# Maxima stored as eight rows, spread by a matmul for the second batch, and a new opening order, in an attention and feed-forward kernel

## The chip, the cores and the metric

The kernel runs on one core of a Trainium2 chip. The metric is the time of one execution on the device in microseconds (us); three executions of the kernel before were timed, and one more was profiled.

## What is computed

Eight batches of eight heads, 576 tokens, head size 64, go through an attention over 32 "memories" per head, and the result goes through a feed-forward network whose two weight matrices arrive as 64-bit floats.

```python
a = exp(phi - max(phi, axis=2)); a = a / sum(a, axis=2)      # phi: 8 x 8 x 576 x 32, over the tokens
k_m, v_m = a^T k, a^T v                                        # 32 memories per head
attn = softmax(q k_m^T / 8)                                    # over the 32 memories
x = (attn v_m), heads side by side: 4608 x 512
h = x @ w_in                                                   # 512 x 2048
out = (h * clip(h + 3, 0, 6) / 6) @ w_out                      # 2048 x 512
```

## The kernel before

**The tiling.** The product of a batch's `v_m` with `w_in` is formed once for each batch (`fold`, four chunks of 512 columns), so that the first large matmul multiplies softmax probabilities with it. The work after that is cut into slots, one for each batch and each 128 of the 2048 columns. A slot has the words `g` (12 matmuls into the tile `ph`, L427), `u` (ACT: relu of h + 3, L437), `m` (DVE: clip and product, L443), `h` and `l` (split of the result into a high and a low part, ACT L456 and DVE L461) and `a` (12 matmuls into the tile `acc`, L481). Slots 0 to 7 are "plain" halves with 4 records for `g` and 4 for `a`. From slot 8 on there are 12, so slot 20 begins with the 177th record of L427 (32 + 12 x 12 + 1), and slot 40, the first that the steady table lays out, with the 369th (slots 36 to 39 have no `g`).

**The order.** Nothing is scheduled by the machine. The string `BEGIN` lists words one after another for slots 0 to 39 of the first two batches; `play` calls the function of each word, and each call appends its instructions to the queue of its engine. Every engine works its own queue strictly in that order. From slot 40 on the table `STEADY` gives the same pattern for each batch. All loads and stores are issued on SP's queue; there too a transfer that must wait holds up all that follow it.

**The attention words** that matter here, with batch and half behind them: `pt`, `pn` load the two layouts of phi (the tiles `ptile` and `pnat`), `kv` a piece of keys and values, `q` the queries. `mx` takes the maxima over the tokens on DVE (L220). Batch 0 spreads them to all partitions on chip: `md` makes two diagonal matrices on DVE (L236), `me` multiplies them by ones on PE (L240). Batches 1 to 7 go through DRAM: `mo` stores the 128 x 2 maxima (L225), `sp` loads them into every partition (L230) and must wait until `mo` has landed. `xa` adds the negated maxima to `pnat` (DVE, L245), `xe` is the exponential (ACT, L249), `kvm` the memories (PE, L257), `nr`, `nk`, `tp`, `tk` normalise and turn them, `sc` the scores (PE, L295), `ct`, `cm`, `cs`, `ex`, `ds`, `dr`, `dm`, `bt` the softmax (`cs` subtracts the maximum, L325; `dm` multiplies by the inverse sum, L337; both on DVE for the first half of batch 0, else on POOL), `bh` and `bl` split the probabilities (`bl`: L350, DVE or POOL as for `cs`). `fo` is the fold (PE, L362), `vc`, `vh`, `vl` copy and split it.

**The weight words.** Weights come as raw 64-bit words (`raw` for a 512 KB piece of `w_in`, `raw2` for a 1 MB unit of `w_out`) and are turned into 32-bit floats by `ab` (ACT, L132), `ro` (ACT, L136), `cl` (DVE, clamp, L140), `sh` (DVE, shift, L143), `si` (DVE, sign, L148) and a final add, which is `tg` on POOL or `to` on DVE (both L158). `sx` and `sy` split a unit of `w_out` into a high part (ACT, L165) and a low part (POOL, L169). `wk` keeps a finished chunk of `w_in` in DRAM. The pieces of `w_in` for chunks 1 to 3 and the pieces of keys and values share one ring of five buffers. `warm` is a matmul that does no work.

Of the kernel before, what the change touches and what calls it, by code (L numbers as in the profile page):

```python
# [729 lines left out]
```

## Time and profile before

| what | us |
|---|---|
| three timed executions, median (lowest to highest) | 755.34 (751.94 to 755.71) |
| the profiled execution, its own time | 754.04 |
| its span, first to last instruction | 752.2 |
| PE busy in it | 718.6 |
| DVE busy | 390.7 |
| ACT busy | 325.8 |
| POOL busy | 113.1 |

PE is busy for 96% of the span, but that share is an average. From some 140 us on it is at work without a gap; before that it waits. Rows of a timeline give the start, the length and the engine of an instruction, and in brackets how long its engine had been idle and what ended that.

### The profile page before, as it was taken

The page shows a single profiled execution, that of the slowest core. Times are in us where ns is not written, and L with a number is a line of the kernel's source. Part 1 is how long each engine was busy: PE and PEld are TensorE (multiplying, and loading weights), DVE is VectorE, ACT ScalarE, POOL GpSimd, SP SyncE. Part 2 cuts the span into 40 slices and gives each one's busy share as a digit, 9 for nine tenths or more (in the row PEclk, how much of TensorE's full clock was granted, in tenths as well). Part 3 has the DMA queues.
Part 4 walks back from the last instruction along what each step waited for, and adds up shares of the span by engine and source line. Part 5 has one row for each costly group of instructions (what it writes and reads, how often), then busy time and mean ns, then how long its engine had stood idle before and what let it go on. Part 6 is the DMA issues. An engine that isn't in the chain of part 4 may idle for free.

```text
span 752.2 us, 11547 instructions
## 1 busy us (share of the span) xinstructions
PE 718.6 (96%) x4754; PEld 565.6 (75%) x4758; DVE 390.7 (52%) x576; ACT 325.8 (43%) x625; POOL 113.1 (15%) x74
## 2 busy tenths in 40 slices
PE   7886958999999999999999999999999999999997
PEld 3334637778887878787887878787887878888885
DVE  3897878675635355345543354444543455343332
ACT  2565646555433344443443434343433434343331
POOL 1352633133200021002200021002200022000000
PEclk9998998999999999999999999999999999999999
DMA  9948873549523080816263080816264211130002
GB/s 322 408 49 317 244 226 135 202 140 229 190 83 126 15 332 3 154 58 247 86 69 143 16 320 13 144 69 218 117 49 161 72 57 57 57 112 1 1 1 70
DMA packets 26453, 99.85 MB, mean 133 GB/s; under 512 B 4513, under 2 KB 5409, under 8 KB 21793
## 3 DMA queue, kind: packets, MB, share of 16 engines
q1 hardware_dynamic: 26400, 99.12, 42.8%
q8 instruction: 37, 0.61, 0.3%
q14 instruction: 16, 0.12, 0.1%
HBM read 83.38 MB, written 15.74 MB: 132 GB/s over the span
## 4 chain that ended last, share of the span: by engine, by line
PE 84%; DMA 8%; DVE 5%; issue 1%; ACT 1%; SPq 0%; DVEq 0%; ACTq 0%
PE acc L481 51%; PE ph L427 26%; DMA raw<-in_w 5%; PE pv L362 4%; PE pk L257 2%; DVE tmp L148 2%; DMA pnat<-in_pn 1%; PE psc L295 1%; DMA qh<-in_qt 1%; DVE tmp L140 1%; DVE tmp L143 1%; DVE both L382 0%; DVE gf L443 0%; ACT tmp L132 0%; DVE glo L461 0%
## 5 line engine op out<-in xcount | busy, mean ns | idle before, releaser
L481 PE MATMUL acc<-w,ghi 128*128 128x512 f32 x1120 | 295.2, 401 | 0.0
L481 PEld LDWEIGHTS acc<-w,ghi 128*128 128x128 f32 x1120 | 205.1, 189 | 68.4 <-ACT gf L437 15.1
L427 PE MATMUL ph<-phi,both 128*128 128x256 f32 x992 | 177.1, 300 | 17.5 <-DVE gf L443 11.7
L443 DVE SCALAR_TENSOR_TENSOR gf<-gf,ph 128x576 f32<-128x576 f32 x124 | 93.4, 753 | 191.4 <-ACT gf L437 191.4
L437 ACT ACTIVATE gf<-ph,three 128x576 f32<-128x576 f32 (+2 forms) x132 | 95.8, 726 | 216.6 <-PE ph L427 213.6
L427 PEld LDWEIGHTS ph<-phi,both 128*128 128x128 f32 x992 | 151.5, 190 | 34.2 <-DVE gf L443 14.1
L481 PE MATMUL acc<-w,glo 128*128 128x512 f32 x560 | 158.1, 395 | 0.0
L481 PEld LDWEIGHTS acc<-w,glo 128*128 128x128 f32 x560 | 105.7, 189 | 25.0
L461 DVE TENSOR_TENSOR glo<-gf,ghi 128x512 fp32r<-128x512 f32 x124 | 88.3, 712 | 44.9 <-ACT ghi L456 41.4
L427 PE MATMUL ph<-plo,both 128*128 128x256 f32 x496 | 107.8, 299 | 0.0
L456 ACT CAST ghi<-gf 128x512 fp32r<-128x512 f32 x124 | 76.4, 616 | 13.6 <-PE acc L481 6.7
L427 PEld LDWEIGHTS ph<-plo,both 128*128 128x128 f32 x496 | 81.0, 192 | 0.0
L382 DVE TENSOR_TENSOR both<-pv,both 128x512 fp32r<-128x512 f32 x62 | 42.5, 689 | 48.6 <-ACT both L373 48.6
L325 POOL TENSOR_TENSOR st<-st,mx 128x640 f32<-128x640 f32 (+1 forms) x15 | 21.8, 1457 | 300.1 <-DVE mx L321 293.3
L447 ACT COPY rest<-gf 128x64 f32<-128x64 f32 x124 | 30.2, 245 | 84.1 <-DVE gf L443 84.1
L373 ACT CAST both<-pv 128x512 fp32r<-128x512 f32 x62 | 35.9, 584 | 25.3 <-DVE both L382 17.4
L362 PE MATMUL pv<-w,kvT 64*32 64x512 f32 (+1 forms) x528 | 36.9, 588 | 1.5 <-DVE w L158 1.3
L350 POOL TENSOR_TENSOR plo<-pT,phi 128x640 fp32r<-128x640 f32 (+1 forms) x15 | 22.2, 1478 | 63.3 <-ACT phi L345 63.3
L337 POOL TENSOR_TENSOR st<-st,sm 128x640 f32<-128x640 f32 (+1 forms) x15 | 19.0, 1267 | 63.8 <-DVE sm L333 61.9
L148 DVE SCALAR_TENSOR_TENSOR tmp<-raw,tmp 128x512 uint32<-128x512 uint32 (+1 forms) x24 | 26.4, 1130 | 0.3
L132 ACT ACTIVATE tmp<-raw 128x512 f32<-128x512 f32 (+1 forms) x24 | 19.1, 832 | 15.4 <-DMA raw<-in_w 12.3
L257 PE MATMUL pk<-kvt,pnat 128*32 128x129 f32 (+1 forms) x640 | 21.5, 276 | 2.4 <-ACT pnat L249 1.7
(64 smaller groups left out, 411.8 us busy)
## 6 DMA issues: line engine op xcount, KB each, us to landing
w<-w_kept SPq DMA_DIRECT2D x24, 1024.0 KB, 8.7
kvt<-in_kv SPq DMA_DIRECT2D x32, 516.0 KB, 7.8
raw<-in_w SPq DMA_DIRECT2D x16, 512.0 KB, 10.1
raw<-in_w SPq DMA_DIRECT2D x8, 1024.0 KB, 13.6
out_t<-o SPq DMA_DIRECT2D x16, 512.0 KB, 2.9
pnat<-in_pn SPq DMA_DIRECT2D x8, 640.0 KB, 7.4
qh<-in_qt SPq DMA_DIRECT2D x8, 640.0 KB, 8.5
ptile<-in_pt SPq DMA_DIRECT2D x8, 576.0 KB, 3.9
```

The lines of the kernel that those rows point to most:

```text
L148: nc.vector.scalar_tensor_tensor(size_, high, 0xC0000000, size_, ALU.bitwise_and, ALU.bitwise_or)
L257: nc.tensor.matmul(self.pk[j * M : (j + 1) * M, g, :KV], self.pnat[:rows, t, g * P + j * M : g * P + (j + 1) * M], kvt[:rows, g * NJ + j, ...
L362: nc.tensor.matmul(to[j * M : (j + 1) * M, g, k], self.kvT[rows, g, j * M : (j + 1) * M], chunk[rows, k, j].bitcast(F32), start=True, stop ...
L373: nc.scalar.copy(both[:, 0], self.pv[c][:, :, VC * k : VC * (k + 1)])
L382: nc.vector.tensor_tensor(both[:, 1], src, both[:, 0].bitcast(F32), ALU.subtract)
L427: nc.tensor.matmul(dst, w[:, g, fs], x[:, g * n : (g + 1) * n], start=(i == 0), stop=(i == len(seq) - 1),)
L437: nc.scalar.activation(self.gf, self.h, AF.Relu, bias=three)
L443: nc.vector.scalar_tensor_tensor(self.gf, relu, 6.0, self.h, ALU.min, ALU.mult)
L447: nc.scalar.copy(kept, self.gf[:, self.n - REST :])
L456: nc.scalar.copy(self.ghi[:, : len(self.tiles) * P], self.gated())
L461: nc.vector.tensor_tensor(self.glo[:, :n], self.gated(), self.ghi[:, :n].bitcast(F32), ALU.subtract)
L481: nc.tensor.matmul(accs[self.b, self.rest, k], left[:, t * P : (t + 1) * P], w, start=k in self.first and k not in begun, stop=k in self.l ...
```

## The change

1. Batch 1 no longer stores its maxima and loads them back (`mo.1`, `sp.1` go). It has `md.1` and `me.1` as batch 0 has; the product goes into the PSUM tile that the attention words share, not into one of the four `acc` banks.
2. From batch 2 on, DVE turns the maxima in 32 x 32 blocks (new word `mt`, a transpose of 128 x 64), so that the 256 values lie in four partitions, and `mo` stores them as eight runs of 32 values instead of 256 single values.
3. `cs`, `dm` and `bl` of the first half of batch 0 move from DVE to POOL. Other POOL work moves to DVE: the low parts of `w_out` units 0, 1, 3, 4 and 5 (`syv`), both `bl` of batch 1 (`blv`), one `dm` of batch 2 (`dmv`). Of the final adds, units 1 and 4 of `w_out` go to DVE and units 6 and 7 to POOL; of `w_in` the two halves of chunk 1 trade engines, half 1 of chunk 2 and half 0 of chunk 3 go to POOL.
4. `BEGIN` is written anew: all loads of the opening and all words of slots 0 to 39 stand in another order. The start of the list before and now:

```diff
-pt.0 raw.0.0 raw.0.1 kv.0.0 kv.0.1 pn.0 kv.0.2 kv.0.3 kv.0.4 raw.0.2 q.0.0 mx.0 md.0 warm.14 me.0 ab.0.0.0 xa.0.0
+kv.0.0 raw.0.0 pt.0 raw.0.1 pn.0 kv.0.1 raw.0.2 raw.0.3 kv.0.2 kv.0.3 kv.0.4 mx.0 q.0.0 ab.0.0.0 md.0 warm.25 me.0
...
-            self.aux = [nc.vector if b == 0 and hf == 0 else nc.gpsimd for hf in range(2)]
...
         def maxima(self):
-            self.nmx = sb.tile([P, NG], F32, name="nmx", tag="nmx", bufs=1)
+            self.nmx = maxima[:, ::M]
             nc.vector.tensor_reduce(self.nmx, self.ptile, AX.X, ALU.max, negate=True)
+
+        def maxima_turn(self):
+            self.turned_ = sb.tile([P, NG * M], F32, name="nmxT", tag="nmxT", bufs=1)
+            nc.vector.transpose(self.turned_, maxima)
 
         def maxima_out(self):
             self.row = dram.tile([NG, P], F32, name=f"nmx{self.b}")
-            nc.sync.dma_start(out=self.row.rearrange("g p -> p g"), in_=self.nmx)
+            rows = self.turned_[::M].rearrange("q (g c) -> q g c", g=NG)
+            nc.sync.dma_start(out=self.row.rearrange("g (q c) -> q g c", c=M), in_=rows)
...
         def every(self):
-            self.nmx = bank()[:, : NG * P]
+            self.nmx = (bank() if self.b == 0 else self.psum("pm").rearrange("p g s -> p (g s)"))[:, : NG * P]
             nc.tensor.matmul(self.nmx, ones, self.diag, start=True, stop=True)
...
-        "un": "vh.0.1.2 vl.0.1.2", "max": "mx.0 mo.0", "spread": "sp.0",
+        "un": "vh.0.1.2 vl.0.1.2", "max": "mx.0 mt.0 mo.0", "spread": "sp.0",
...
+        maxima = cpool.tile([P, NG * M], F32, name="maxima")
+        nc.vector.memset(maxima, 0.0)
```

The line numbers of the changed kernel are one to five higher.

SP's queue, the stretch with the second batch's loads, before (`nmx_442` is the store of the maxima, `nmxb` the load that spreads them, `raw_3` a unit of `w_out`, `kvt` the second batch's keys and values):

```order
L225 DMA nmx_442<-nmx 128x2x1
L199 DMA qh<-in_qt 128x1024
L124 DMA raw_3_446<-in_w 128x1024
L187 DMA pnat<-in_pn 128x1280
L230 DMA nmxb<-nmx_442 128x256
L193 DMA kvt<-in_kv 128x1032 x4
```

and now (`w_kept_72` is the store of the finished chunk 0 of `w_in`):

```order
L125 DMA raw_2_315<-in_w 128x1024
L162 DMA w_kept_72<-w_202 128x2048
L188 DMA pnat<-in_pn 128x1280
L125 DMA raw_3_341<-in_w 128x1024
L200 DMA qh<-in_qt 128x1024
L194 DMA kvt<-in_kv 128x1032
L200 DMA qh<-in_qt 128x1280
L194 DMA kvt<-in_kv 128x1032 x3
```

The store and the load that waits for it are gone; the store of chunk 0 has come forward, and three of the `kvt` loads now stand directly behind the queries.

DVE's queue around the second batch's maxima being added to `pnat`, before (ISA rows are the final adds, `gp` rows the word `m` of a plain slot):

```order
L443 SCALAR_TENSOR_TENSOR gp_489<-gf_466,ph1_80 128x320
L158 ISA w1_474<-raw_389,tmp_435 128x1024
L158 ISA w1_474<-raw_433,tmp_435 128x1024
L140 TENSOR_SCALAR tmp_459<-tmp_459 128x1024
L443 SCALAR_TENSOR_TENSOR gp_503<-gf_491,ph0_79 128x320
L143 TENSOR_SCALAR tmp_459<-tmp_459 128x1024
L245 TENSOR_TENSOR pnat_448<-pnat_448,nmxb_450 128x512
L443 SCALAR_TENSOR_TENSOR gp_522<-gf_518,ph1_80 128x320
```

and now (`pm` is the PSUM tile of `me.1`):

```order
L448 SCALAR_TENSOR_TENSOR gp_478<-gf_471,ph0_79 128x320
L448 SCALAR_TENSOR_TENSOR gp_480<-gf_473,ph1_80 128x320
L250 TENSOR_TENSOR pnat_331<-pnat_331,pm_450 128x512 x2
L159 ISA w1_475<-raw_198,tmp_441 128x1024
L159 ISA w1_475<-raw_208,tmp_441 128x1024
L250 TENSOR_TENSOR pnat_331<-pnat_331,pm_450 128x256
L448 SCALAR_TENSOR_TENSOR gp_510<-gf_490,ph0_79 128x320
```

The addition reads the product of the matmul instead of the loaded tile, and the add that gives back two ring buffers stands behind it instead of in front.

POOL's queue up to slot 0, before (two halves of chunk 0's final add, `cs` of the second half):

```order
L158 TENSOR_TENSOR w_262<-tmp,raw 128x512 x2
L325 TENSOR_TENSOR st<-st,mx 128x640
L158 TENSOR_TENSOR w_262<-tmp,raw 128x512 x2
L158 TENSOR_TENSOR tmp<-tmp,raw_0_260 128x1024
L337 TENSOR_TENSOR st<-st,sm 128x640
```

and now:

```order
L159 TENSOR_TENSOR w_202<-tmp,raw 128x512 x4
L330 TENSOR_TENSOR st<-st,mx 128x512
L330 TENSOR_TENSOR st<-st,mx 128x640
L342 TENSOR_TENSOR st<-st,sm 128x512
L342 TENSOR_TENSOR st<-st,sm 128x640
L159 TENSOR_TENSOR tmp<-tmp,raw_0_163 128x1024
```

All four pieces of chunk 0's add are now in front of the softmax of batch 0, and the softmax of its first half has joined this queue.

## Rows read from the trace of the kernel before

**Rows 1.** Stages: length, busy of PE, PEld, DVE, ACT, POOL (us), clock, DMA share, GB/s
```profile
0.00:31.36 31.36, 25.51 (x210) 11.19 (x214) 16.45 (x31) 12.42 (x20) 6.04 (x10) 1.00 0.96 361
31.36:63.46 32.10, 23.06 (x91) 11.05 (x92) 27.60 (x33) 19.13 (x31) 16.02 (x9) 0.95 0.68 195
63.46:141.20 77.74, 64.71 (x471) 49.18 (x471) 64.79 (x84) 47.68 (x86) 30.55 (x16) 0.93 0.72 229
141.20:235.06 93.86, 92.95 (x575) 74.62 (x574) 51.81 (x74) 40.05 (x77) 18.32 (x10) 1.00 0.43 133
235.06:752.20 517.14, 512.42 (x3411) 419.57 (x3409) 230.08 (x357) 206.52 (x412) 42.15 (x30) 1.00 0.34 100
```
**Rows 2.** Timeline of SP's queue around the first store of the maxima
```profile
44.16 0.39 SPq L225 DMA_DIRECT2D nmx<-nmx  x1
53.09 0.33 SPq L230 DMA_DIRECT2D nmxb<-nmx  x1
```
**Rows 3.** The same around the second store
```profile
91.47 0.38 SPq L225 DMA_DIRECT2D nmx<-nmx  x1
100.59 0.33 SPq L230 DMA_DIRECT2D nmxb<-nmx  x1
```
**Rows 4.** Stages read for their DMA rate (last column), columns as in rows 1
```profile
24.00:36.00 12.00, 9.84 (x55) 4.90 (x56) 11.86 (x18) 8.47 (x14) 5.20 (x4) 1.00 1.02 418
45.00:53.00 8.00, 7.40 (x21) 3.40 (x19) 7.86 (x12) 7.09 (x13) 2.65 (x3) 1.00 0.85 40
92.00:100.00 8.00, 5.71 (x29) 4.29 (x27) 7.93 (x9) 4.05 (x7) 5.81 (x3) 1.00 0.96 33
```
**Rows 5.** Timelines after the first store: ACT, DVE, PE
```profile
60.21 1.10 ACT L136 ACTIVATE raw<-raw 128x1024 uint32<-128x1024 uint32 x1 [8.12 <-DMA raw<-in_w]
62.22 0.69 DVE L245 TENSOR_TENSOR pnat<-pnat,nmxb 128x512 f32<-128x512 f32 x1 [3.67 <-DMA nmxb<-nmx]
63.46 0.77 PE L427 MATMUL ph<-phi,both 128*128 128x256 f32 x2 [5.54 <-DVE gp L443]
```
**Rows 6.** Timeline of DVE after the second store
```profile
110.20 0.69 DVE L140 TENSOR_SCALAR tmp<-tmp 128x1024 f32<-128x1024 f32 x1 [5.13 <-ACT tmp L132]
```
**Rows 7.** DVE's groups from 31.36 to 141.20: busy us, mean ns, idle before
```profile
L140 DVE TENSOR_SCALAR tmp<-tmp 128x1024 f32<-128x1024 f32 x14 | 17.2, 1227 | 7.0 <-ACT tmp L132 7.0
L148 DVE SCALAR_TENSOR_TENSOR tmp<-raw,tmp 128x512 uint32<-128x512 uint32 x12 | 13.2, 1141 | 0.2
L158 DVE CUSTOM_DVE_ANT_0 w<-raw,tmp 128x1024 uint16<-128x1024 uint16 x6 | 5.6, 979 | 0.0
```
**Rows 8.** Timeline of DVE, the same instructions while POOL is idle, and `cs`
```profile
14.33 0.69 DVE L140 TENSOR_SCALAR tmp<-tmp 128x1024 f32<-128x1024 f32 x1
15.78 1.29 DVE L148 SCALAR_TENSOR_TENSOR tmp<-raw,tmp 128x512 uint32<-128x512 uint32 x2
22.81 0.69 DVE L325 TENSOR_TENSOR st<-st,mx 128x512 f32<-128x512 f32 x1
...
103.79 1.28 DVE L158 CUSTOM_DVE_ANT_0 w<-raw,tmp 128x1024 uint16<-128x1024 uint16 x2
```
**Rows 9.** POOL's groups from 31.36 to 141.20, columns as in rows 7
```profile
L169 POOL TENSOR_TENSOR w<-tmp,w 128x1024 fp32r<-128x1024 f32 x5 | 13.6, 2712 | 1.4 <-ACT w L165 1.4
L158 POOL TENSOR_TENSOR w<-tmp,raw 128x512 uint32<-128x512 uint32 x8 | 12.5, 1585 | 19.0 <-DVE tmp L148 12.5 <-ACT raw L136 6.5
L158 POOL TENSOR_TENSOR tmp<-tmp,raw 128x1024 uint32<-128x1024 uint32 x4 | 10.8, 2705 | 37.4 <-DVE tmp L148 19.8 <-DMA raw<-in_w 14.4 <-ACT both L377 1.9
...
L325 POOL TENSOR_TENSOR st<-st,mx 128x512 f32<-128x512 f32 x1 | 1.5, 1493 | 0.0
```
**Rows 10.** PE's timeline in the opening
```profile
17.83 0.64 PE L257 MATMUL pk<-kvt,pnat 64*32 64x129 f32 x16 [0.72 <-DMA kvt<-in_kv]
```
**Rows 11.** DMA issues over the whole span: KB each, median us to landing
```profile
out_t<-o SPq DMA_DIRECT2D x8, 128.0 KB, 2.3
```
**Rows 12.** Timeline of DVE in slot 40
```profile
241.66 0.68 DVE L245 TENSOR_TENSOR pnat<-pnat,nmxb 128x512 f32<-128x512 f32 x1
```

More of the change, by code (lines that the diff above doesn't have):

```diff
@@ new lines @@
+ro.0.0.0 q.0.1 xa.0.0 cl.0.0.0 xe.0.0 xa.0.1 raw2.0 warm.8 kvm.0.0 xa.0.2 kvm.0.1 sh.0.0.0 xe.0.2 raw2.1 xe.0.1
+si.0.0.0 raw.1.0 ro.0.0.1 tg.0.0.0 ab.0.0.1 raw.1.1 warm.10 kvm.0.2 cl.0.0.1 warm.5 kvm.0.3 sh.0.0.1 warm.1 kvm.0.4
+nr.0 si.0.0.1 nk.0 warm.5 tp.0 tk.0 tg.0.0.1 warm.2 sc.0.0 sc.0.1 ct.0.0 pt.1 raw.1.2 fo.0.0.0 cm.0.0 raw.1.3 ct.0.1
+raw2.2 cs.0.0 wk.0 cm.0.1 ex.0.0 ab.1.0 cs.0.1 ds.0.0 dr.0.0 cl.1.0 ex.0.1 pn.1 dm.0.0 ab.1.1 ds.0.1 sh.1.0 vc.0.0.0
+raw2.3 bt.0.0 ro.1.0 warm.24 fo.0.0.1 dr.0.1 g.0 q.1.0 si.1.0 vc.0.0.1 g.1 u.0 dm.0.1 m.0 kv.1.0 mx.1 u.1 g.2 ro.0.1.0
@@ new lines @@
+tg.1.0 m.1 q.1.1 bt.0.1 u.2 warm.2 g.3 ab.0.1.1 m.2 cl.1.1 a.0 u.3 md.1 ro.1.1 cl.0.1.1 sh.1.1 a.1 ab.1.2 sh.0.1.1 m.3
+ab.0.1.0 si.1.1 g.4 bh.0.1 cl.0.1.0 me.1 ro.1.2 to.1.1 g.5 bh.0.0 sh.0.1.0 a.2 sx.0 si.0.1.1 ro.0.1.1 a.3 si.0.1.0 u.4
+u.5 tg.0.1.1 m.4 m.5 g.6 k.4 ro.1.3 xa.1.0 xa.1.1 g.7 u.6 k.5 to.0.1.0 xe.1.1 a.4 xe.1.0 u.7 bl.0.0 xa.1.2 kv.1.1
+ab.1.3 m.6 kv.1.2 fo.0.1 kv.1.3 cl.1.2 k.6 kv.1.4 bl.0.1 m.7 a.5 raw2.6 vh.0.1.0 vl.0.1.0 cl.1.3 vh.0.1.1 hb.1 g.8
+xe.1.2 sh.1.2 vl.0.1.1 si.1.2 kvm.1.0 u.8 kvm.1.1 raw.2.0 k.7 m.8 kvm.1.2 raw.2.1 sh.1.3 h.8 kvm.1.3 to.1.2 kvm.1.4
@@ new lines @@
+m.13 h.12 g.14 e.11.0 l.12 e.11.1 raw.3.1 e.11.2 q.2.1 sh.0.2.1 fo.1.1 eo.11.0 e.11.3 si.0.2.1 raw.3.2 h.13 a.12
+vh.1.1.0 k.12 tg.0.2.1 u.14 k.13 m.14 ro.0.3.0 vl.1.1.0 g.15 xa.2.1 ab.0.3.0 raw.3.3 kv.2.0 l.13 raw2.5 k.14 cl.0.3.0
+a.13 u.15 ab.1.4 m.15 sh.0.3.0 vh.1.1.1 xa.2.2 h.14 vl.1.1.1 h.15 g.16 l.14 ab.0.3.1 l.15 si.0.3.0 fo.0.2 u.16 a.14
+cl.0.3.1 vh.0.2.0 tg.0.3.0 vh.0.2.1 xe.2.2 vl.0.2.1 k.15 ro.1.5 m.16 vl.0.2.0 k.16 xe.2.0 g.17 kv.2.1 sh.0.3.1 ab.1.6
+kv.2.2 cl.1.4 raw2.7 si.0.3.1 ro.0.3.1 eo.11.1 kvm.2.0 a.15 xe.2.1 tg.0.3.1 u.17 m.17 k.17 g.18 h.16 sh.1.4 kv.2.3
@@ L165, in split_high, with split_low @@
         nc.scalar.copy(w2_sb[u][:, 0], sizes[1, u].bitcast(F32))
-    def split_low(u):
+    def split_low(u, engine=None):
         whole = sizes[1, u].bitcast(F32)
-        nc.gpsimd.tensor_tensor(w2_sb[u][:, 1], whole, w2_sb[u][:, 0].bitcast(F32), ALU.subtract)
+        (engine or nc.gpsimd).tensor_tensor(w2_sb[u][:, 1], whole, w2_sb[u][:, 0].bitcast(F32), ALU.subtract)
     def w2_parts(f):
@@ L333, in invert, with divide @@
             nc.vector.reciprocal(sm, sm)
-        def divide(self, hf):
+        def divide(self, hf, engine=None):
             st = self.by_token(hf)
-            self.aux[hf].tensor_tensor(st, st, self.over_memories(hf, "sm"), ALU.mult)
+            (engine or nc.gpsimd).tensor_tensor(st, st, self.over_memories(hf, "sm"), ALU.mult)
         def back(self, hf):
@@ L595, in attention_ffn_kernel @@
     ATTENTION = {
-        "mx": A.maxima, "mo": A.maxima_out, "sp": A.spread, "md": A.diagonal, "me": A.every, "xa": A.less_max,
+        "mx": A.maxima, "mt": A.maxima_turn, "mo": A.maxima_out, "sp": A.spread, "md": A.diagonal, "me": A.every, "xa": A.less_max,
         "xe": A.phi_exp, "kvm": A.memories, "nr": A.weights, "nk": A.normalise, "tp": A.turn, "tk": A.turned,
         "sc": A.scores, "ct": A.scores_turn, "cm": lambda a, hf: a.reduce(hf, "mx"), "cs": A.centre,
+        "csv": lambda a, hf: a.centre(hf, nc.vector), "dmv": lambda a, hf: a.divide(hf, nc.vector),
+        "blv": lambda a, hf: a.back_low(hf, nc.vector),
         "ex": A.exponent, "ds": lambda a, hf: a.reduce(hf, "sm"), "dr": A.invert, "dm": A.divide, "bt": A.back,
```

62 lines of the change are left out of this document (24 added, 38 removed).

## The prediction

> **What bounds the kernel now.** I read the stages first. From slot 20 on (141.20 us) PE is busy for 92.95 of 93.86 us, then for 512.42 of 517.14 [rows 1]: there the kernel is its matmuls, and nothing that ends on another engine can shorten it. Before that PE has gaps. [...] So from slot 0 (31.36) to slot 20, in 109.84 us, DVE works 92.39 and is idle 17.45. DVE is the tightest engine of this stretch, and the rest of it is waiting. What I look for is where that idle time ends, and why DVE's work takes so long.
>
> Second, SP's queue. The store of the second batch's maxima goes out at 44.16; the load that needs it follows at 53.09, 8.9 us later [rows 2]. The next batch repeats this, 91.47 to 100.59 [rows 3]. This is no mere latency: with loads already queued behind, the DMAs move 40 and 33 GB/s while these stores are under way, and 418 GB/s in the opening [rows 4]. A store of 1 KB, in 256 single values, blocks the queue for some nine us each time.
>
> Third, who pays. After the first store ACT has stood 8.12 us for a piece of weights, DVE 3.67 us for the spread maxima, and PE 5.54 us for DVE [rows 5]. After the second, DVE stands 5.13 us for ACT's magnitudes [rows 6], whose raw weights were issued behind the waiting load.
>
> Fourth, DVE's work itself. The clamp takes 1227 ns on average in this stretch, the sign 1141, the final add 979 [rows 7]; with POOL idle they take 690, 645 and 640 (half of a row of two) [rows 8].
>
> **The change, part by part.** All of it is set against the profiled execution, 754.0 us, which is 1.3 below the median of the timed ones.
>
> *The opening, to slot 0: +0.5.* The last piece of keys and values now stands behind two more 512 KB pieces of weights, 0.52 MB each, so 1.25 us apiece at 418 GB/s [rows 4]. PE waited for that very piece at 17.83 [rows 10], so the scores come about 2.5 us later. Against that, the first half's weight work (a clamp, a shift, two signs) leaves DVE's chain behind the scores; other weight work takes part of its place, worth about -2.5. `cs` on POOL takes 1.49 us for 0.69 on DVE [rows 9, 8], `dm` likewise, and both queue behind chunk 0's adds: +1 or less. The nearest ends are -2 (all of the weight work hidden) and +4 (the late keys and POOL's queue in full). I take +0.5, as the opposing parts nearly cancel.
>
> *The first store goes: -3.7.* I take DVE's idle time, not PE's 5.54 or ACT's 8.12, since DVE is the engine without slack here [rows 5]. What comes next is DVE's own work. `md.1` and `me.1` cost DVE half a microsecond and PE about as much, and the product is there long before `pnat`, so they lie beside other work. Bounds: -1 (ACT's work becomes late instead) and -8.1 (ACT's wait).
>
> *The second store shrinks: -5.1.* Eight runs of 128 B in place of 256 of 4 B. The trace has no such store. The nearest from above is the store it replaces, 8.9; from below the small final store, 2.3 us for 128 KB [rows 11]. I take 2.3, since that has few long runs and the new one fewer still: the load of maxima is then issued some 6.6 us sooner, the weights behind it too, and DVE's 5.13 us [rows 6] go. Bounds 0 and -6.6. In the later batches the same saving lies under PE, which has no gap there: 0.
> [...]
>
> *POOL's work to DVE: -4.8.* Between slots 0 and 20 POOL loses four low parts of 2.71 us, two adds of 2.71 and one `bl` of about 1.5, and gains one half chunk of two pieces of 1.59: -14.6 us of the 46.6 that it works there [rows 9, 1]. DVE's lengthening, from the three rows that I can price, is 14 x 0.54 + 12 x 0.50 + 6 x 0.34 = 15.6 us, or 0.33 us for each us of POOL's. So -14.6 x 0.33 = -4.8; ends 0 (POOL's other work lengthens it as much) and -8.
> The work itself lands on DVE: four low parts at about 1.28 us (the row nearest to it is the final add's, two pieces [rows 8]), one `bl` and the small words, together about +6.5. As much leaves: the clamp, shift, sum and reciprocal that now stand ahead of slot 0 (2.6) and three clamps, a shift and a sign that now stand behind slot 20 (4.0), where DVE is busy for only 51.81 of 93.86 us [rows 1]. Net 0, ends -2 and +3.
> [...]
>
> *The clock: -2.* A share of 0.95 and 0.93 [rows 1] is 0.05 x 32.1 + 0.07 x 77.7 = 7.0 us of PE time given away after gaps. Fewer gaps give some back, but DVE hides most: ends 0 and -7.
>
> *A new wait: +1.* Three of the loads of keys and values wait for buffers that chunk 1's adds free, and one of these adds now stands on DVE behind the spread maxima. By 2.3 us for a small transfer [rows 11] and 1.25 for each of three and a half pieces they land six to seven us after it, and PE wants them right after slot 8, which can begin some three us after that add and takes two to three. Ends 0 and +7.
>
> *Slot 40: 0.* The third `sp` is now the last issue ahead of slot 40. Its tile is wanted at 241.66 [rows 12], some six us after slot 40 begins; if it is late, DVE has slack in that stage. Ends 0 and +2. The transposes, one a batch, lie under PE: 0.
>
> The sum: 0.5 - 3.7 - 5.1 - 4.8 + 0 - 2 + 1 + 0 = -14.1, so 754.0 - 14.1 = **739.9, say 740**.
>
> **The rivals.**
> *The ring sets the loads* (748). If keys and values, and then the weights behind them on SP, still wait for buffers, the new wait is at its end of +7 and part of the second store's gain goes too: 740 + 6 + 2 = 748. For it speaks that the ring has five buffers before and after; against it, that the wait for the store is out of the queue. At its farthest, every wait gone is a shadow of this one, and little but the contention is won: 753.
> *VectorE is the floor* (732). If all of DVE's 17.45 us of idle time goes, and 4.8 with it: 754.0 - 22.3 = 732. PE's busy time from slot 0 to slot 20, 87.8 us, would allow it. Against it, DVE, ACT and PE hand each other every slot.
> *The store stays slow* (745). If the price is by the run of less than some length, not by the count of runs, the second store still takes 8.9 and its 5.1 us stay: 745. The second batch's still goes.
> *Slower* (760). One mechanism: the add of chunk 1 that frees two buffers (DVE) stands behind the maxima from `me.1`, which stands on PE behind slot 4, and SP's whole queue stands behind those buffers. Every us that this add ends late is a us for all later loads. Before, the keys and values went out behind the load of maxima at 53.09 [rows 2]. If the add ended near 78, they would be there at about 84.5; PE now begins slot 8 at 63.46 [rows 5] and is through it and the memories some 5.5 us later. That is 15.5 us late, against 9.9 that the second store and POOL's work still win: 754.0 + 15.5 - 9.9 = 760. It decides against the change once the add ends after about 72. DVE's work ahead of that add sums to about 50 us by my count, which speaks against it.
>
> **How the numbers follow.** Forecast 740: 0.52. Ring 748: 0.15, and its far end 753: 0.07. Floor 732: 0.13. Slow store 745: 0.07. Slower: 0.06. About 0.5% (3.8 us) is what a measurement of this kernel can tell from no change, so "same" is 751.6 to 759.1. Faster: 0.52 + 0.15 + 0.13 + 0.07 = 0.87; same 0.07; slower 0.06. The range 730 to 751 holds the forecast with its bounds, the ring, the floor and the slow store; it leaves out the two last cases (0.13) and the outer edges of the others.
>
> **What would show it.** Right: no idle DVE in front of `xa.1`; the store of the third batch's maxima landing in under 4 us, and no stretch at 40 GB/s; slot 8 at 54 to 58 us for 63.46, slot 20 at 124 to 130 for 141.20; a mean clamp nearer to 0.9 us; slots 20 to 40 as long as before. Wrong: slot 0 after 35, ACT or PE standing for `raw` or `kvt` for over 4 us after slot 8, or a gap of PE in slots 40 to 42.

## The result, and the profile after

The changed kernel takes **723.11 us** (median of four runs, 722.99 to 723.91) against 754.81 in four runs of the kernel before beside it: a ratio of 0.9588, with an interval of 0.9561 to 0.9616. The forecast was 740 with a range of 730 to 751: the direction was right, but the time lies 7 us below the range, and the gain is 31.7 us where 14.1 were forecast. Slot 8 begins at 52.06 us and slot 20 at 114.53, both earlier than the signs that the prediction named (54 to 58, 124 to 130). The profiled execution took 722.99, its span is 721.2.

The stages after, each cut where slots 0, 8, 20 and 40 begin (columns as in rows 1):

```profile
0.00:30.68 30.68, 27.21 (x229) 11.30 (x229) 17.57 (x34) 13.35 (x21) 10.05 (x13) 1.00 0.95 354
30.68:52.06 21.38, 20.72 (x84) 11.02 (x77) 21.05 (x34) 18.46 (x32) 11.71 (x6) 1.00 0.98 379
52.06:114.53 62.47, 60.57 (x505) 45.80 (x503) 56.55 (x82) 45.35 (x82) 22.20 (x14) 1.00 0.72 250
114.53:205.58 91.05, 91.05 (x542) 73.68 (x543) 55.47 (x81) 42.54 (x80) 19.44 (x10) 1.00 0.44 159
205.58:721.20 515.62, 510.95 (x3411) 417.45 (x3409) 229.94 (x359) 206.57 (x412) 42.22 (x30) 1.00 0.27 98
```

Beside [rows 1], stage by stage: to slot 0 -0.7 us, slots 0 to 20 -26.0 (109.84 to 83.85), slots 20 to 40 -2.8, the rest -1.5; together the 31.0 by which the span is shorter. In slots 0 to 20 PE was busy for 87.77 us and stood for 22.1; now it is busy for 81.29 and stands for 2.6. The 6.5 us of busy time fell away although PE has more records there (589 for 562); the granted clock was 0.95 and 0.93 before, with 0.50 in stretches of 2 us in and behind PE's gaps (61.36 to 65.36, 111.36 to 113.36, 125.36 to 127.36), and is 1.00 now in every stretch of 2 us. What PE waited for in this stretch, first before (31 to 142 us), then after (30 to 115); the columns are total, times, longest:

```profile
PE ph L427 <- DVE gf L443: 11.7, 4, 5.3
PE ph L427 <- DVE gp L443: 8.0, 4, 5.5
PE pv L362 <- DVE w L158: 1.3, 2, 0.6
```
```profile
PE ph L432 <- DVE gf L448: 1.2, 2, 1.0
PE psc L300 <- ACT kvT L288: 0.5, 1, 0.5
PE pv L367 <- DVE pnat L250: 0.5, 1, 0.5
PE ph L432 <- DVE gp L448: 0.2, 1, 0.2
```

PE's waits for the plain and the later slots' DVE words, nearly 20 us, have shrunk to 1.4. PE is now the bound of this stage too; with PE's work as it is, no more than 2.6 us are left in it.

The stores. SP's queue at the third batch's maxima, which answers to [rows 3]:

```profile
72.07 0.65 SPq L230 DMA_DIRECT2D nmx<-nmxT  x1
73.77 0.33 SPq L235 DMA_DIRECT2D nmxb<-nmx  x1
```

The load that must wait for the store follows it after 1.7 us; it was 9.1. No other transfer stands between the two here; the case with loads in the queue is e1, below. And DVE around the second batch's maxima, which answers to DVE's row in [rows 5]:

```profile
44.41 0.86 DVE L448 SCALAR_TENSOR_TENSOR gp<-gf,ph 128x320 f32<-128x320 f32 x2
45.21 1.27 DVE L250 TENSOR_TENSOR pnat<-pnat,pm 128x512 f32<-128x512 f32 x2
46.41 2.73 DVE L159 CUSTOM_DVE_ANT_0 w<-raw,tmp 128x1024 uint16<-128x1024 uint16 x2
```

No bracket stands behind the addition at 45.21: DVE came to it without a pause, 17 us earlier than before.

DVE's groups from slot 0 to slot 20 (as rows 7) and the POOL groups that matter (as rows 9):

```profile
L141 DVE TENSOR_SCALAR tmp<-tmp 128x1024 f32<-128x1024 f32 x10 | 9.7, 975 | 0.0
L149 DVE SCALAR_TENSOR_TENSOR tmp<-raw,tmp 128x512 uint32<-128x512 uint32 x12 | 7.6, 681 | 0.1
...
L159 POOL TENSOR_TENSOR w<-tmp,raw 128x512 uint32<-128x512 uint32 x10 | 16.1, 1628 | 29.3 <-DVE tmp L149 26.6 <-ACT raw L137 2.6
L159 POOL TENSOR_TENSOR tmp<-tmp,raw 128x1024 uint32<-128x1024 uint32 x2 | 4.9, 2436 | 0.0
...
L170 POOL TENSOR_TENSOR w<-tmp,w 128x1024 fp32r<-128x1024 f32 x1 | 2.4, 2444 | 9.9 <-ACT w L166 9.9
```

The clamp's mean went from 1227 to 975 ns, the sign's from 1141 to 681, close to the 645 with POOL idle [rows 8]. On POOL the long instructions (those on 1024 columns) fell from nine to three in this stretch [rows 9].

### The profile page after: what moved, and what is told of

It is laid out like the page before. It is cut to its first block, busy times and chain, and to the rows that moved or that the text cites. A ratio compares the mean times of both kernels' runs of the same rounds, so it can differ in the third digit from the quotient of the medians.

```text
span 721.2 us, 11545 instructions
## 1 busy us (share of the span) xinstructions
PE 710.5 (99%) x4758; PEld 559.3 (78%) x4758; DVE 380.6 (53%) x586; ACT 326.3 (45%) x625; POOL 105.6 (15%) x73
## 4 chain that ended last, share of the span: by engine, by line
PE 90%; DVE 4%; DMA 3%; issue 1%; POOL 1%; ACT 1%; SPq 0%; ACTq 0%; POOLq 0%
PE acc L486 55%; PE ph L432 27%; PE pv L367 4%; PE pk L262 2%; DMA qh<-in_qt 2%; DMA pnat<-in_pn 1%; PE psc L300 1%; PE acc L584 1%; DVE gf L448 1%; DMA raw<-in_w 1%; DVE glo L466 0%; POOL w L170 0%; DVE tmp L141 0%; DVE tmp L149 0%; ACT gf L442 0%
## 5 line engine op out<-in xcount | busy, mean ns | idle before, releaser
L432 PE MATMUL ph<-phi,both 128*128 128x256 f32 x992 | 172.8, 296 | 1.4 <-DVE gf L448 1.2
L432 PEld LDWEIGHTS ph<-phi,both 128*128 128x128 f32 x992 | 149.1, 188 | 16.9 <-DVE gf L448 3.8
L432 PE MATMUL ph<-plo,both 128*128 128x256 f32 x496 | 105.7, 294 | 0.0
L330 POOL TENSOR_TENSOR st<-st,mx 128x512 f32<-128x512 f32 (+1 forms) x16 | 22.8, 1426 | 291.5 <-DVE mx L326 291.5
L367 PE MATMUL pv<-w,kvT 64*32 64x512 f32 (+1 forms) x528 | 35.1, 588 | 0.5 <-DVE pnat L250 0.5
L355 POOL TENSOR_TENSOR plo<-pT,phi 128x512 fp32r<-128x512 f32 (+1 forms) x14 | 21.2, 1522 | 56.6 <-ACT phi L350 56.6
L342 POOL TENSOR_TENSOR st<-st,sm 128x512 f32<-128x512 f32 (+1 forms) x15 | 19.6, 1305 | 64.7 <-DVE sm L338 52.9
L159 POOL TENSOR_TENSOR w<-tmp,raw 128x512 uint32<-128x512 uint32 x14 | 21.8, 1577 | 46.6 <-DVE tmp L149 39.6
L584 PE MATMUL acc<-rest,ident 128*128 128x512 bf16 x82 | 21.7, 415 | 1.7 <-DVE rest L679 1.7
## 6 DMA issues: line engine op xcount, KB each, us to landing
qh<-in_qt SPq DMA_DIRECT2D x8, 640.0 KB, 10.2
```

The lines of the kernel that those rows point to most:

```text
L367: nc.tensor.matmul(to[j * M : (j + 1) * M, g, k], self.kvT[rows, g, j * M : (j + 1) * M], chunk[rows, k, j].bitcast(F32), start=True, stop ...
L432: nc.tensor.matmul(dst, w[:, g, fs], x[:, g * n : (g + 1) * n], start=(i == 0), stop=(i == len(seq) - 1),)
L584: nc.tensor.matmul(fill["out"], ident.bitcast(BF16)[:, :P], fill["in"], start=True, stop=True)
```

## The experiments

The theories that the runs are to tell apart: **stores** (the transfers won it), **engines** (POOL's work moved to DVE won it, by less lengthening of DVE's work), **order** (the new list itself won it). Start of a slot in each profile, in us, and the median:

| kernel | slot 0 | slot 8 | slot 20 | slot 40 | median | ratio to before (95%) |
|---|---|---|---|---|---|---|
| before | 31.36 | 63.46 | 141.20 | 235.06 | 754.81 | 1 |
| after | 30.68 | 52.06 | 114.53 | 205.58 | 723.11 | 0.9588 (0.9561, 0.9616) |
| e15, the changed code with the old order, engines and stores | 30.92 | 62.67 | 141.35 | 234.89 | 752.10 | 0.9974 (0.9961, 0.9988) |
| e1, stores alone | 31.59 | 60.09 | 132.28 | 225.82 | 742.88 | 0.9841 (0.9812, 0.9871) |
| e3, engines alone | 35.50 | 68.10 | 145.11 | 242.61 | 758.71 | 1.0065 (1.0042, 1.0088) |
| e4, all but the order | 35.08 | 66.43 | 136.26 | 233.75 | 751.62 | 0.9969 (0.9952, 0.9987) |
| e6, all but the engines | 31.34 | 58.29 | 122.57 | 214.72 | 732.07 | 0.9702 (0.9671, 0.9733) |
| e5, all but the small stores | 30.18 | 51.56 | 117.44 | 208.50 | 732.90 | 0.9718 (0.9696, 0.9741) |
| e7, low parts on POOL | 30.83 | 54.04 | 119.54 | 211.99 | 727.76 | 0.9651 (0.9630, 0.9672) |
| e9, batch 1 by way of DRAM | 30.37 | 54.40 | 116.91 | 207.99 | 725.83 | 0.9631 (0.9605, 0.9656) |
| e10, new order to slot 8 | 30.38 | 53.22 | 129.56 | 227.07 | 743.63 | 0.9855 (0.9831, 0.9878) |
| e11, new order from slot 8 | 36.04 | 67.25 | 129.59 | 220.61 | 737.93 | 0.9781 (0.9763, 0.9798) |
| e12, e4 with the first half on DVE | 31.41 | 62.89 | 132.37 | 229.53 | 746.72 | 0.9889 (0.9870, 0.9908) |
| e8, before with short POOL instructions | 31.26 | 63.29 | 139.63 | 232.41 | 750.72 | 0.9955 (0.9935, 0.9974) |
| e13, after with short POOL instructions | 30.18 | 51.70 | 114.27 | 205.72 | 724.81 | 0.9606 (0.9587, 0.9624) |

All runs of this table but e8 are made from the changed code, so e15, which has nothing of the three, is the run to set them beside. It is 2.3 us faster than the kernel before; the last group of runs comes back to that.

The next table is a count over DVE's instructions from slot 0 to slot 20: for each, its time beyond the median of its form and shape over these traces (**lengthening**), that median (**free work**), and the idle time in front of it (**waits**). Records that follow each other overlap a little, so the three add up to some 7 to 9 us more than the stretch.

| us | before | e1 | e3 | e4 | e6 | e7 | e8 | e10 | e11 | after |
|---|---|---|---|---|---|---|---|---|---|---|
| free work | 80.1 | 80.7 | 84.9 | 85.6 | 75.3 | 76 | 81.3 | 83.7 | 82.4 | 80.5 |
| lengthening | 18.9 | 19.0 | 12.6 | 12.8 | 12.5 | 11.0 | 15.3 | 9.0 | 9.1 | 5.9 |
| waits | 17.5 | 8.2 | 20.0 | 10.9 | 11.7 | 10.2 | 19.2 | 15.7 | 9.5 | 6.2 |

**The stores.** e1 keeps the old order and engines; batch 1 still goes through DRAM, every batch with the store of eight rows.

```diff
-mo.1
+mt.1 mo.1
...
-mo.2
+mt.2 mo.2
```

> The old order and the old engines; only the store of the maxima is turned and has eight rows, for batches 1 to 7; batch 1 still goes through DRAM. If the two blocked stretches of about nine us cost what VectorE stood idle behind them (3.7 and 5.1), the time is about 745 to 747, and no stretch of the opening moves 40 GB/s with loads queued. If the order hides them (buffers of the ring come free no sooner), it is 752 or more. If the eight-row store is slow as well, the store's landing stays near 9 us and the time at 754.

Slot 20 comes 8.9 us earlier. DVE's lengthening is the same as before, its waits are 9.3 shorter. The two stages of e1, beside [rows 1], and SP's queue in it, which answers to [rows 2]:

```profile
31.59:60.09 28.50, 23.20 (x92) 11.04 (x92) 27.82 (x35) 20.04 (x32) 16.06 (x9) 1.00 0.62 237
60.09:132.28 72.19, 64.80 (x470) 48.87 (x471) 64.70 (x85) 47.05 (x85) 30.57 (x16) 0.93 0.67 242
```

```profile
46.47 0.66 SPq L230 DMA_DIRECT2D nmx<-nmxT  x1
...
48.62 1.18 SPq L235 DMA_DIRECT2D nmxb<-nmx  x1
```

The store is out of the way in 2.2 us for 8.9, among the same loads. What the old store did to them shows in the load of queries issued right behind it, before and in e1:

```profile
L199 SPq DMA_DIRECT2D qh<-in_qt x1: 413/413/413, 44.6 to 44.6; - x1
DMA to landing us min/median/max: 12.5/12.5/12.5
```
```profile
L200 SPq DMA_DIRECT2D qh<-in_qt x1: 334/334/334, 47.2 to 47.2; - x1
DMA to landing us min/median/max: 4.5/4.5/4.5
```

All seven stores of 256 values in the kernel before land 8.5 to 9.3 us after their issue.

e5 puts the store of 256 values back into the changed kernel, for batches 2 to 7.

```diff
-            rows = self.turned_[::M].rearrange("q (g c) -> q g c", g=NG)
-            nc.sync.dma_start(out=self.row.rearrange("g (q c) -> q g c", c=M), in_=rows)
+            nc.sync.dma_start(out=self.row.rearrange("g p -> p g"), in_=self.nmx)
```

> The new order and engines, batch 1 by the matmul, but the maxima of batches 2 to 7 stored as 256 single values again. If the block of about nine us is no longer hidden, VectorE stands for the third batch's spread maxima and ScalarE for chunk 3's weights: 727 to 732. If the new order gives those loads enough room (they wait for buffers anyway), 723 to 725.

It costs 9.8 us, at two places. SP's queue, then DVE and PE, in slots 40 to 42 of e5:

```profile
203.86 0.58 SPq L229 DMA_DIRECT2D nmx<-maxima  x1
...
215.84 0.34 SPq L234 DMA_DIRECT2D nmxb<-nmx  x1
```
```profile
219.88 0.69 DVE L249 TENSOR_TENSOR pnat<-pnat,nmxb 128x512 f32<-128x512 f32 x1 [4.71 <-DMA nmxb<-nmx]
...
222.70 1.22 PE L431 MATMUL ph<-phi,both 128*128 128x256 f32 x4 [4.06 <-DVE gf L447]
```

The third `sp` stands last ahead of slot 40, and with a store of 12 us it is late there; the other place is a wait of DVE of 3.36 us at 81.88, which puts slot 20 back by 2.9 us. From slot 40 on e5 loses 6.9 us, more than PE's wait of 4.06: the granted clock is 0.89 from 208.50 to 240 us, and the four `ph` records that took 0.63 us at 214.09 take 1.22 behind that wait. So the order was free to put `sp.3` last only because of the small store.

e9 lets batch 1 store and load its maxima in the changed kernel.

```diff
+mt.1 mo.1 sp.1
...
-md.1
...
-me.1
```

> The change with batch 1 spread through DRAM, its store of eight rows and its load standing directly behind its maxima, in place of the diagonal and the matmul. The store is issued into a queue with ten us of loads in front and the load of maxima behind it, so if the matmul is what the opening needs, VectorE stands some 5 us in front of the second batch's additions: 727 to 731. If the eight-row store alone is enough, 722 to 725.

It costs 2.7 us. Here the store goes out at 34.05 and the load only at 44.53, but that is another thing than [rows 4] show: in these 10.5 us the DMAs move 382 GB/s. Here the small store stands in line behind loads that keep moving; the old one held up those behind it (the queries landed after 12.5 us, for 4.5 in e1).

**The engines.** e3 has nothing but the moves between POOL and DVE, in the old order with the old stores; e4 adds the stores and the matmul for batch 1; e6 is the changed kernel with the old engines.

```diff
-sy.0 sy.1 sy.3 sy.4 sy.5 bl.1.0 bl.1.1 dm.2.1
+syv.0 syv.1 syv.3 syv.4 syv.5 blv.1.0 blv.1.1 dmv.2.1
-tg.1.1 tg.1.4 to.1.6 to.1.7 tg.0.1.0 to.0.1.1 to.0.2.1 to.0.3.0
+to.1.1 to.1.4 tg.1.6 tg.1.7 to.0.1.0 tg.0.1.1 tg.0.2.1 tg.0.3.0
```

(`cs.0.0`, `dm.0.0` and `bl.0.0` go to POOL as well.)

> The old order and the old stores; only the engines of the additions, the low parts, and the first batch's softmax steps are those of the change. Theory: a clamp or sign on VectorE waits out the POOL instruction that is running when it is issued, so what counts is the length of the POOL instructions that it meets, and the four low parts of 2.7 us that leave POOL take most of the long waits with them: VectorE's mean clamp falls from 1.23 to below 1.0 us and the time to 748 to 752, since VectorE has the moved work to do. Rival, lengthening in proportion to POOL's busy time: about -4.8 against +6.5 of moved work, 754 to 757. Third theory, the order alone brings the fall in lengthening: the mean clamp stays at 1.2 us and the time at 755 or more.

> The old order with all else of the change: eight-row stores, maxima of the second batch spread by the matmul (its two words stand behind the second batch's maxima and behind slot 4, and the other two additions of the maxima behind the first), the engines of the change. If stores and engines make the gain, 728 to 738. If the new order makes most of it, 742 to 748.

> The new order and stores, with every addition, low part and softmax step on the engine that it had before. Theory of long POOL instructions: the mean clamp rises again to 1.2 us or more and the time to 729 to 735. Rival, the order alone: clamp and time stay, 721 to 726.

The lengthening falls by 6.3 us in e3, as the moves should make it, and the time does not follow: it is 4.4 us longer than before, 6.6 longer than in e15. From slot 0 to slot 20 DVE has 4.8 us more work of its own and 2.5 us more waits, so the stretch stays as long as it was (109.61 us for 109.84). The loss lies ahead of slot 0, 4.1 us, and in slots 20 to 40, 97.50 us for 93.86; what makes the second was not taken apart. PE in e4, and POOL in e3 ahead of slot 0:

```profile
53.31 1.01 PE L486 MATMUL acc<-tmp,gp 128*128 128x512 f32 x1 [2.81 <-DVE tmp L159]
```
```profile
22.07 1.05 POOL L329 TENSOR_TENSOR st<-st,mx 128x512 f32<-128x512 f32 x1 [20.76 <-DVE mx L325]
23.07 2.52 POOL L159 TENSOR_TENSOR w<-tmp,raw 128x512 uint32<-128x512 uint32 x2
...
31.36 1.50 POOL L341 TENSOR_TENSOR st<-st,sm 128x512 f32<-128x512 f32 x1
```

PE waits for an add that went to DVE; and the first half's `dm` ends at 32.86 on POOL, so slot 0 starts at 35.50. e12 tests the second point: e4 with these three words back on DVE.

```diff
-cs.0.0 dm.0.0 bl.0.0
+csv.0.0 dmv.0.0 blv.0.0
```

> The run with all but the order, with the first batch's first softmax half (maximum subtracted, inverse sum multiplied, low part) back on VectorE. Slot 0 began at 35.1 us there and at 31.4 before. If POOL's queue in front of these steps is the cause, slot 0 comes back to 31 to 32 and the time to 746 to 749. If not, 751.

Slot 0 is back at 31.41, the whole 4.9 us faster than e4. In the new order the same moves are worth 9.0 us (e6 to after), over half of it the five low parts:

```diff
-syv.0 syv.1 syv.3 syv.4 syv.5
+sy.0 sy.1 sy.3 sy.4 sy.5
```

> The change with the five low parts of the second weight matrix back on POOL, nothing else moved. VectorE loses 5 x 1.2 us of work and meets five more POOL instructions of 2.7 us. If the lengthening decides, it rises by some 5 us between slots 0 and 20 and the time is 725 to 729. If VectorE's work decides, 720 to 723.

e7 is 4.7 us slower than the changed kernel, and its lengthening 11.0 for 5.9. But its free work is 4.5 us less, so the two nearly cancel; the stretch from slot 0 to slot 20 is 4.9 us longer, and it is DVE's waits that are longer, 10.2 us for 6.2.

**The order.** e10 has the new list up to slot 8 and the rest in the old order, e11 the other way round; both have the stores and engines of the change. The changed list and that of e10 where they part:

```diff
-vh.0.1.1 hb.1 g.8 xe.1.2 sh.1.2 vl.0.1.1 si.1.2 kvm.1.0 u.8 kvm.1.1
+vh.0.1.1 hb.1 g.8 raw2.4 syv.0 sx.1 sh.1.2 vl.0.1.1 xe.1.2 sh.1.3 u.8
```

> Stores, matmul spread and engines of the change; the new order up to slot 8's first matmuls, then the remaining words in the old order. Against the run with all but the order (751.6; slot 8 at 66.4 us, slot 20 at 136.3), the new opening is worth 14 us at slot 8. If that is a gain of its own it stays to the end: 736 to 740. If the words behind it wait for what the old order loads late, 744 or more.

> The other half: the old order up to slot 8, then the new one. The stretches from slot 8 to 20 and from 20 to 40 are 7.4 and 6 us shorter in the change than in the run with all but the order; if the order behind slot 8 does that by itself, 737 to 741. If it needs the earlier loads, 745 or more.

From e4 the opening alone wins 8.0, the rest alone 13.7, both 28.5: 6.8 belong to neither. e10 is 13 us ahead of e4 at slot 8 and gives half of it back before slot 20; in the old order behind it PE waits for ACT and DVE again:

```profile
63.28 0.68 PE L284 MATMUL pq<-ident,kvn 128*128 128x128 f32 x2 [2.64 <-ACT kvn L279]
...
97.00 0.88 PE L432 MATMUL ph<-phi,both 128*128 128x256 f32 x4 [3.19 <-DVE gf L448]
```

e6 beside e1 shows that the order alone also lowers the lengthening, 19.0 to 12.5, with POOL as busy as before (43.2 and 46.6 us).

**POOL's instructions.** What lengthens DVE's work? A clamp of DVE and the POOL instruction beside it, in the kernel before:

```profile
54.72 2.83 DVE L140 TENSOR_SCALAR tmp<-tmp 128x1024 f32<-128x1024 f32 x1
```
```profile
54.20 2.80 POOL L169 TENSOR_TENSOR w<-tmp,w 128x1024 fp32r<-128x1024 f32 x1
```

POOL's ends at 57.00, the clamp at 57.55, 0.55 us later, though alone it takes 0.69 in all. Two further pairs of that trace read the same: POOL to 89.63 and the clamp to 90.18, POOL to 126.82 and the clamp to 127.37. The clamp waits out what POOL has begun, and it is not alone. Counted in the traces from slot 0 to slot 20, these DVE instructions began beside a running POOL instruction, were lengthened and ended 0.55 us after it, none more than 0.01 us off; beside them, what of the lengthening is theirs:

| | before | e1 | e3 | e6 | e8 | after |
|---|---|---|---|---|---|---|
| instructions | 15 | 15 | 11 | 10 | 17 | 7 |
| their lengthening, us | 17.7 | 17.9 | 9.8 | 11.8 | 13.6 | 5.1 |

They are clamps, shifts, signs, adds and subtractions that read both inputs, or their only one, from SBUF. Transposes, reductions and the word `m`, which reads PSUM, kept their time beside POOL: the maxima took 1.34 us at 42.80 beside POOL and 1.34 at 90.10 without it; in the changed kernel a transpose of 128x640 took 0.84 at 34.28 beside it and 0.84 at 72.13 without; `gp` at 44.55, in the midst of a POOL instruction, took 0.49 us, and 0.47 at 57.47 without one. e8 tests the length of the POOL instruction: the kernel before, with POOL's instructions on 1024 columns cut in two, the same work in shorter pieces (the final adds of `w_out` in the same way as the low parts shown).

```diff
...
-        nc.gpsimd.tensor_tensor(w2_sb[u][:, 1], whole, w2_sb[u][:, 0].bitcast(F32), ALU.subtract)
+        for cols in (slice(0, FC), slice(FC, UNIT)):
+            nc.gpsimd.tensor_tensor(
+                w2_sb[u][:, 1, cols], whole[:, cols], w2_sb[u][:, 0, cols].bitcast(F32), ALU.subtract
+            )
```

> The kernel before; POOL's instructions of 1024 columns (low parts, and final adds of the second matrix) are cut into two of 512 each, the same work in the same place. Theory: a VectorE instruction that needs what POOL holds waits until the POOL instruction that is running ends, so with instructions half as long the waits on them halve: some 4 to 6 us less lengthening between slots 0 and 20, the time 748 to 752. Rival, lengthening in proportion to POOL's busy time: unchanged or a little up, 754 to 757.

```profile
L140 DVE TENSOR_SCALAR tmp<-tmp 128x1024 f32<-128x1024 f32 x14 | 11.6, 828 | 7.5 <-ACT tmp L132 7.5
L148 DVE SCALAR_TENSOR_TENSOR tmp<-raw,tmp 128x512 uint32<-128x512 uint32 x12 | 11.0, 958 | 0.2
```

With POOL busy for longer (50.2 us for 46.6) the clamp falls from 1227 to 828 ns, and the kernel is 3.8 us faster. A price in proportion to POOL's busy time would have made it slower. The gain is about the least that a measurement of this kernel can tell, but its interval lies below 1. DVE meets POOL as often as before, but the longest meetings are gone. Not all of it becomes time: the lengthening is 3.6 us less, the waits 1.7 us more, and slots 0 to 20 are 1.5 us shorter. The same cut in the changed kernel gains nothing (724.81): of the three long instructions left there, none is met by one of the seven above.

> The change with POOL's remaining instructions of 1024 columns cut into two of 512. VectorE's lengthening between slots 0 and 20 is 5.5 us there, a third of it behind long POOL instructions: 721 to 723 by the theory that a VectorE instruction waits out the running POOL instruction; 723 to 725 if the additional instructions cost more than that.

**Where the tiles lie.** A steady slot takes 4.400 us in the kernel before (slots 54, 55 and 56 begin at 306.02, 310.43 and 314.82) and in e8, and 4.38 to 4.39 in everything made from the changed code but e17. e14 is the kernel before plus the new tile `maxima`, unused; e15 the changed code with old order, engines and stores; e16 the kernel before with the small tile `nmx` 16 columns wide; e17 the changed kernel with a tile of two columns more in that place, which DVE sets to zero once a batch. The edits of e14, e16 and e17:

```diff
+        maxima = cpool.tile([P, 64], F32, name="maxima")
+        nc.vector.memset(maxima, 0.0)
...
-            self.nmx = sb.tile([P, NG], F32, name="nmx", tag="nmx", bufs=1)
+            self.nmx = sb.tile([P, 16], F32, name="nmx", tag="nmx", bufs=1)[:, :NG]
...
+            odd = sb.tile([P, NG], F32, name="odd", tag="odd", bufs=1)
+            nc.vector.memset(odd, 0.0)
```

> The kernel before, with nothing but the changed kernel's new constant tile (128 x 64 floats, set to zero, not read by anything). Open is why a steady slot takes 4.400 us in the trace before (slots 54 to 56: 306.02, 310.43, 314.82) and in the run with POOL's instructions cut in two, but 4.385 in every kernel that was made from the changed code, whatever its order, stores and engines; over the steady stage that is 1.6 to 1.8 us. Theory: where the tiles lie in SBUF (the new tile shifts all that follow) sets it: steady slots of 4.385, the stage from slot 40 to the end near 515.4 instead of 517.1, the whole some 1.5 us below the kernel before, slot 20 within half a microsecond of 141.20. Rival: it comes from something the changed program does (the maxima written into every 32nd column, its names and words): slots of 4.400, the whole equal to before.

> The changed kernel's code with the old order, the old engines and the old stores: all that is left of the change is the new tile, into every 32nd column of which the maxima are written and from which the 256 values are stored. Theory of the layout: like the run with the tile alone, steady slots of 4.385 and the stage from slot 40 near 515.4, the whole some 1.5 us below before. Rival, that the writing or storing of the maxima from the new tile does it: 4.385 here and 4.400 with the tile alone. If both are 4.400, the difference belongs to the new order or engines, against the run with the engine moves alone, which had 4.385. Slot 20 at 141.2 within one microsecond by all theories.

> The kernel before, in which the small tile of the maxima is 16 floats wide (64 bytes in each partition) and only its first two columns are used, as before. Nothing else is changed. The run with the new tile alone left the steady slots at 4.400 us, the one that also gives up the small tile has 4.385. Theory: the small tile of 8 bytes shifts every tile laid out behind it by an odd amount, and the shift costs PE 0.3%: slots of 4.385 here, the stage from slot 40 near 515.4, the whole some 2 us below before. Rival: the maxima's use of the new tile, not the place of the others, does it: slots of 4.400, the whole equal to before.

> The changed kernel with a tile of two floats a partition put back where the small tile was; it is set to zero by DVE once a batch and never read. Theory of the shift: steady slots go from 4.385 to 4.400, the stage from slot 40 from 515.6 to 517 or more, the whole some 2 us above the changed kernel (725). Rival: slots stay at 4.385, the whole at 723 to 724 (eight settings to zero of well under 0.2 us each).

e14: 754.67, slots of 4.400, ratio 1.0001 (0.9992, 1.0010). e15: 752.10, 4.380, 0.9974 (0.9961, 0.9988). e16: 752.96, two thirds of the slots at 4.38 and the rest at 4.40, 0.9979 (0.9965, 0.9992). e17: 721.93, slots of 4.36, 0.9563 (0.9549, 0.9577). A change of one tile's width alone (e16) moves most steady slots, so the place of the tiles seems to play a part; no run shows how. The theory of an odd shift falls: in e17 the odd tile made the slots shorter, not longer. Which tile and which place matter is open. From slot 40 to the end e17 takes 514.0 us, the changed kernel 515.6, the kernel before 517.1. e17 is thus the fastest of all, by 1.2 us, less than the 0.5% that a measurement can tell and with an interval that overlaps the changed kernel's.

## Where the prediction failed, and what of it was right

The terms for the stores held. The term for the lengthening was too small by 8.2 us, and the new order, worth 10.8 us beside e1 and 28.5 beside e4, had no term.

*The stores: right.* The forecast had -3.7 and -5.1, in sum -8.8. In e1 slots 0 to 8 are 3.6 us shorter and slots 8 to 20 5.5, slot 20 comes 8.9 earlier, and beside e15, the same code with the old stores, the whole is 9.2 us faster (742.88 and 752.10). Taking DVE's idle time as the price, not PE's or ACT's, held. That the store stays slow, the third rival, is out: in e1 the load follows the eight runs of 128 B after 2.2 us, in the changed kernel after 1.7.

*The failed step* is "POOL's work to DVE: -4.8", with its price of 0.33 us for each us of POOL's. DVE's lengthening fell by 13.0, from 18.9 to 5.9. POOL's busy time fell only from 46.6 to 33.9 us, so a price in proportion would give -4.2. Two things stand in its place. The price is per meeting: a clamp (or a sign, a shift, an add) of DVE that starts beside a running POOL instruction ends 0.55 us after it, 15 times before and 7 times now, so that what counts is how many meet and how long POOL's instruction is; e8 shows the second. Why DVE's instruction waits there, no run shows. And the new order keeps the two apart: e6 against e1 has 6.5 less, in 10 meetings for 15, with POOL's work nearly unchanged. The moves (-6.3, e3) and the order (-6.5) make -12.8 of the -13.0.

*The term that was missing* is the order itself, the fourth part of the change: the sum had only +0.5, +1 and 0 for its ends. Taken in steps from e15, the stores win 9.2 us (e1), the order 10.8 more (e6, which also has batch 1's matmul), the engines 9.0 more; the stores and engines without the order win 0.5 in all (e4). Between e1 and e6 DVE's free work in slots 0 to 20 falls by 5.4 us and its lengthening by 6.5, while its waits rise by 3.5; the stretch is 9.5 us shorter.

*The moved work: net 0.* About right for the whole change (free work 80.1 to 80.5), but the reason was the order: it takes as much work out of the stretch as the moves bring in. In the old order the moves add 4.8 and lose (e3).

*The clock: -2.* Mis-sized. I let DVE hide most of it; with PE standing 2.6 us for 22.1 the granted clock is 1.00 from slot 0 on, and PE's busy time is 6.5 us shorter, near the end of -7. These 6.5 us are PE's side of the same 26.0, in which DVE's lengthening and waits are counted too; the two accounts are not to be added.

*The new wait: +1.* Wrong in sign, without weight. SP does stand for the ring from 34.4 to 45.67, but the keys and values land some 7 us after their issues, and PE takes them at 54.14 without a wait.

*The opening: +0.5.* It was -0.7. POOL's queue costs nothing in the new order; e12 shows that in the old order it costs 3.7 us at slot 0.

*Slot 40: 0.* Right (`xa.3` runs without a wait), but only with the small store, as e5 shows. *Slots 20 to 40 as long as before:* wrong by 2.8. PE's busy time there fell from 92.95 to 91.05, in 542 records for 575, and its idle time from 0.9 to 0; 0.3 us of this is in e15 already (93.54), and the larger part seems to be work that stands ahead of slot 20 now. *The steady stage, no term:* -1.5; e15, with none of the three in it, has it too (515.4 us for 517.1).

Miss by miss, if a microsecond of lengthening counts as one of time, as the prediction took it: lengthening 8.2, what is left of slots 0 to 20 3.2, slots 20 to 40 2.8, the steady stage 1.5, the opening 1.2; together the 16.9 us between a span shorter by 31.0 and a forecast of 14.1. That rate is not shown: in e8 3.6 us less lengthening came with a stretch 1.5 us shorter, in e3 6.3 us less, beside 4.8 of moved work, with one no shorter. How much of the 8.2 is time stays open; what is measured is that the lengthening fell by 13.0 and that the stretch is 26.0 us shorter. The nearest rival was the floor of VectorE (732). It let DVE's waits go in full; in truth 6.2 of 17.5 stayed, and the lengthening, which it left at the forecast's size, fell by 13.0.

## What to carry to other kernels

Where one engine lengthens another's instructions, do not price the share of busy time: look for single instructions that end together (here 0.55 us apart, 15 times before and 7 after), and count the meetings and the length of the longest. The store of 1 KB in 256 single values was costly by the queue that it stopped for 8.9 and 9.1 us, with 40 and 33 GB/s moved, not by its bytes; look at the rate of all DMAs while it is under way, and at when the loads behind it land. Work moved to another engine and the order of the work are one change: the same moves lost 4.4 us in the old order (6.6 beside e15) and won 9.0 in the new.

## What the runs showed of the hardware

DVE's clamp, alone 0.69 us, took up to 2.86 beside one POOL instruction of 2.90; 15 DVE instructions of the kernel before, four clamps among them, ended 0.55 us after the POOL instruction beside which they began, and that is 17.7 of 18.9 us of lengthening. POOL's instructions on 1024 columns took 2.39 to 3.26 us in that stretch, the three left in the changed kernel 2.42 to 2.46. A store of 256 single values took 8.5 to 9.3 us in the kernel before, and the DMAs moved 40 and 33 GB/s beside the first two, with loads queued behind; eight rows of 128 B let the load follow in 1.7 (the changed kernel, at 72.07) to 2.2 (e1), or, behind loads under way at 382 GB/s, in 10.5 (e9). And the steady slot, which nothing in the change touches, took between 4.36 and 4.40 us with one small tile wider, added or left out.
